# Expert 0's second matrix measured inside the attention, layer 2 in a written order, and 16 identity matmuls ahead of its first rows

## The chip, the core and the metric

The kernel runs on one core of one Trainium2 chip. Its engines are PE (TensorE, the matmuls), DVE (VectorE), ACT (ScalarE), POOL (GpSimd) and SP (SyncE, which here only issues transfers). The metric is the device time of one run in microseconds (us). The profile is one execution, recorded instruction by instruction.

## The reference, cut to what matters

Three stages follow one another: a sparse attention and two mixtures of experts.

```python
# attention: 2 batches, 8 heads, 768 positions, 64 wide, scores kept for 96 local and 8 global positions
scores = scale * q @ k^T + bias;  a = softmax(scores where kept);  x = a @ v      # x: 1536 x 512

# first mixture (called the dense layer): all 8 experts see all 1536 rows, D = 512, F = 1024
P = exp(logits - max)
for _ in range(8):                          # the balancing of the probabilities
    P /= P.sum(1);  P /= P.sum(0);  P *= N / E
out += P[:, e] * (max(x @ w1[e], 0) @ w2[e])          # over e

# second mixture (called layer 2): each expert takes 192 rows, assigned greedily by logit
out[mask_e] = max(x[mask_e] @ w1[e], 0) @ w2[e]
```

## The kernel before

**Numbers and products.** Each float32 operand of the large products is split into two float16 parts, a high and a low one: ACT writes the high part (`split_hi`, L814) and DVE the low one (`split_lo`, L817), both scaled by a power of two that comes from the operand's largest absolute value. A product is then three matmuls (`mm3`, L869 to L871): high by high, high by low, low by high. A matrix of an expert (512 x 1024 or 1024 x 512) must therefore be loaded, measured for its maximum, given a scale, and split before PE can use it. To find a maximum over all partitions, a column of 128 maxima is sent through PE (`spread`, L134, or a transpose of a broadcast column) and reduced.

**Attention.** `band_attention` runs in a written order: inside `with in_order():` each instruction of an engine is tied behind the one before it in the program's text, so that the program's order is the order of the engine's queue. It goes in steps, two per block of 128 rows and 12 blocks. Beside its blocks it runs generators that are asked for one item at fixed places of each step. One of them is `matrices()` (L558), which calls `matrix(0)` (L525): it loads expert 0's first matrix as two transfers of 1 MB into the two buffers of the pool tag `raw`, reduces it in eight parts on DVE (L539, steps 2 to 5), gets its scale by `want_scale` and `broadcast`, and splits it in eight parts on ACT, DVE and POOL (steps 8 to 11). Scores of a step come from PE (`scores`, L595) after DVE's copy of the turned keys into a slab (L584); DVE and ACT then do the softmax (`soften`, L599). From step 13 on, some of expert 0's first products (x by its first matrix) are done inside the attention.

**Between attention and dense layer.** After the attention (about 156 us) the remaining first products of expert 0 follow in nine groups of 12 products of 512 columns each. Behind each group side streams are pumped: small work of other engines (loading, measuring, splitting of weights) is issued in units with a cost for ACT, DVE and POOL. Stream `weights` (L1217) loads expert 0's second matrix in four quarters, measures it in eight parts, four on ACT (`absmax_bound`, L883) and four on DVE (L1202) in `measured`, then settles its scale in `settle` (reduction L1209, spread L134 on PE), and splits it. In the same time the probabilities are balanced on DVE and POOL (L909 to L925). The four quarters of raw space are `quarters`, views of the two `raws`.

**Dense layer.** From 186 us to about 1137 us, in a written order: output products of expert 0 (`out_step`, the 512-column products of L1464), then experts 1 to 7, with the side streams that prepare each next matrix pumped behind fixed groups of products.

**Layer 2.** The dense layer's rows and gate logits give an assignment `inv` of rows to places. The layer's largest absolute value is broadcast by PE (L119), and the rows go out to `xg` in DRAM. Then four pairs of experts follow. For each pair, POOL gathers 384 rows from `xg` (`load_rows`), PE turns them in three sets of four transposes (`turn_rows`, L1956) and ACT and DVE split them. Each expert's first products are four groups of 24 products of 192 columns (`ph`, L869 to L871), evicted by `split_relu` (two passes on ACT, L862 and L863, and one on DVE, L864). Output products (`py`) are 24 products of 512 columns over 8 row blocks f, one per expert and one more for the shared remainder (L2035), each evicted on ACT or DVE and scattered by POOL. PE's groups write to four banks in turn.

Eight of the 16 matrices of layer 2 were split earlier and stored in DRAM (`NPRE = 8`); `fetch` brings them back whole. The other eight are made in layer 2 itself: `make` loads a matrix in eight pieces of 128 x 512 into a ring of five places in `raw2` (POOL issues the first five, SP the others at L1979) and splits each with `split`. This part of the program is not written in a fixed order: the scheduler of the program's builder sets the place of each instruction in each engine's queue.

Of the kernel before, what the change touches and what calls it, by code (L numbers as in the profile page):

```python
# [42 lines left out]
def tile_sparse_attention_moe_moe(ctx, tc, q, k, v, ng, nl, wg1, w11, w12, wg2, w21, w22, out, taps=None):  # L43
# [64 lines left out]

    late = []
# [286 lines left out]
    def band_attention(atp, aps):  # L396
# [161 lines left out]
        def matrices():  # L558
            yield from matrix(0)

# [393 lines left out]
    raws = [rawp.tile([P, WE // 2], F32, name="raw", bufs=2) for _ in range(2)]  # L954
# [262 lines left out]
    def weights(jobs):  # L1217
# [693 lines left out]
    sx2 = pow2_scale(xam[:, NC:], "sx2")  # L1911
    xg = drp.tile([NT, DM], F32)
# [37 lines left out]
    def turn_rows(a):  # L1950
        xr = XR.pop(a)
        x2 = xtp.tile([P, 2, KC, 3 * P], F16, name="xt")
        for z in range(3):
# [4 lines left out]
            last = nc.scalar.activation(hi, pt, AF.Copy, scale=sx2[:, 0:1])  # L1958
            nc.vector.scalar_tensor_tensor(lo, pt, sx2[:, 0:1], hi, op0=ALU.mult, op1=ALU.subtract)
        X2[a] = x2, inv[:, 3 * a:3 * a + 3]  # L1960
        return last

    raw2 = lat.tile([P, NC * DM], F32, name="raw2", tag="acc", bufs=1)
    spare = raw2.bitcast(F16)[:, :2 * 2 * FC * CAP].rearrange("p (z y f t) -> p z y f t", z=2, y=2, f=FC)
    ring = [raw2[:, 2 * FC * CAP + 512 * y:2 * FC * CAP + 512 * y + 512] for y in range(5)]
    turn_ = [0]

    def make(e, which):
        kind, n = seq[USES.index((e, which)) % len(seq)]
        t = pools[kind, n].tile([P, 2, WE], F16, name="w2slot", tag=f"{kind}{n}", bufs=1)  # L1970
        w = (w21, w22)[which][e]
        for a in range(8):
            raw = ring[turn_[0] % len(ring)]
            turn_[0] += 1
            c, h = divmod(a, w.shape[1] // 512)
            if turn_[0] <= len(ring):
# [90 lines left out]
```

## Time and profile before

| | |
|---|---|
| median of 3 runs | 1300.54 us (1300.19 to 1301.31) |
| the profiled execution's own time | 1300.56 us |
| its span, first to last instruction | 1298.8 us |
| PE busy | 1242.9 us, 96% of the span |
| DVE busy | 889.6 us, 68% |
| ACT busy | 754.3 us, 58% |
| POOL busy | 208.6 us, 16% |
| moved by DMA | 211.39 MB, 163 GB/s on average |

Busy time counts what an engine executes, not register, branch, semaphore and transfer-issuing instructions. A share of the span is an average over stages with different limits; the slices and the windows show where an engine was not full. The clock column (PEclk) is TensorE's granted clock, 1.00 being 2.4 GHz and 0.50 being 1.2 GHz; a window in which it changed shows a value between. A row of a window gives its limits and length, then busy us with the count of instructions for PE, PEld (TensorE's weight loads), DVE, ACT and POOL, then the granted clock, the busy share of the DMA engines and GB/s. A row of a timeline gives start, duration, engine, line, operation, tile written <- tiles read, shape and count, and ends, where the engine idled ahead of it, with that idle time and what released it.

### The profile page before, as it was taken

The numbers are of one execution on the slowest core, as the hardware profiler recorded it, in microseconds if no ns is written. First come the engines' busy times: TensorE is split into PE (matmuls) and PEld (weight loads), VectorE is DVE, ScalarE is ACT, GpSimd is POOL, SyncE is SP. The second block draws the span as 40 slices with busy tenths as digits, with TensorE's granted clock in tenths as the row PEclk, the third lists the DMA queues.
The fourth block names the chain that finished last, engine by engine and source line by source line (L and its number), as shares of the span: only waits on it lengthen the run. The fifth ranks groups of instructions, "written<-read, shape, count | busy, mean of one in ns | idle before, by whom it ended". The sixth has DMA issues, their size and how long they took to land.

```text
span 1298.8 us, 24591 instructions
## 1 busy us (share of the span) xinstructions
PE 1242.9 (96%) x9462; PEld 819.7 (63%) x9462; DVE 889.6 (68%) x2038; ACT 754.3 (58%) x1507; POOL 208.6 (16%) x269
## 2 busy tenths in 40 slices
PE   6899989999999999999999999999999999979997
PEld 4666434685478548897468547855785444467665
DVE  7865586777548645878657765776778898836851
ACT  5876453585356435767448645645574676736852
POOL 2543407203001100201100200110000000041100
PEclk9999989999999999999999999999999999989999
DMA  9440023574832473734787674225745233368740
GB/s 243 109 126 14 2 82 130 193 230 163 275 106 74 130 227 128 248 145 152 243 280 238 208 268 148 74 90 182 256 155 196 94 136 128 114 234 286 248 134 25
DMA packets 157445, 211.39 MB, mean 163 GB/s; under 512 B 56528, under 2 KB 91344, under 8 KB 156048
## 3 DMA queue, kind: packets, MB, share of 16 engines
q1 hardware_dynamic: 154720, 198.02, 47.0%
q0 software_dynamic: 2320, 7.60, 1.6%
q10 hardware_dynamic: 288, 4.19, 0.8%
q8 instruction: 74, 1.21, 0.4%
q14 instruction: 43, 0.35, 0.1%
HBM read 176.23 MB, written 33.55 MB: 162 GB/s over the span
## 4 chain that ended last, share of the span: by engine, by line
PE 72%; issue 10%; DVE 9%; ACT 5%; DMA 2%; POOL 2%; POOLq 0%; DVEq 0%; ACTq 0%; SPq 0%
PE pX L1464 11%; PE pY L1490 10%; PE py L1694 8%; PE pX L1490 7%; PE pY L1464 7%; PE pZ L1464 5%; PE pV L1464 5%; PE pV L1490 4%; PE pZ L1490 3%; DMA raw<-in_moe_w_dram 2%; DVE hslot L1511 2%; PE ph L869 1%; PE ph L871 1%; PE ph L870 1%; PE pr L1816 1%
## 5 line engine op out<-in xcount | busy, mean ns | idle before, releaser
L1490 PEld LDWEIGHTS <-ws 128*128 128x128 f16 x3528 | 344.1, 98 | 44.5 <-issue 1.2
L1464 PEld LDWEIGHTS <-hslot 128*128 128x128 f16 x1776 | 172.4, 98 | 199.3
L1464 PE MATMUL pX<-wslot,hslot 128*128 128x512 f16 x768 | 171.5, 379 | 0.0
L1490 PE MATMUL pY<-xs,ws 128*128 128x256 f16 x1008 | 124.7, 273 | 0.5 <-DVE pZ L1570 0.5
L1490 PE MATMUL pX<-xt,ws 128*128 128x256 f16 x1008 | 124.2, 273 | 0.3 <-ACT pY L1539 0.3
L1694 PE MATMUL py<-wslot,hslot 128*128 128x512 f16 x528 | 121.0, 379 | 0.0
L1511 DVE TENSOR_TENSOR hslot<-relu,hslot 128x512 f16<-128x512 f32 x126 | 97.1, 794 | 31.1 <-ACT relu L1504 30.8
L1288 POOL TENSOR_TENSOR raw<-raw 128x512 f32<-128x512 f32 x14 | 22.9, 1633 | 513.3 <-DVE ws L817 222.2
L814 ACT ACTIVATE ws<-raw,s 128x512 f16<-128x512 f32 x98 | 66.3, 714 | 53.8 <-POOL raw L1296 21.7
L1464 PE MATMUL pY<-wslot,hslot 128*128 128x512 f16 x432 | 96.9, 379 | 0.0
L817 DVE SCALAR_TENSOR_TENSOR ws<-raw,s,ws 128x512 f16<-128x512 f32 x98 | 78.0, 821 | 15.7 <-ACT ws L814 15.5
L1694 PEld LDWEIGHTS <-hslot 128*128 128x128 f16 x528 | 49.4, 99 | 60.6 <-issue 8.3
L883 ACT ACTIVATE wide<-raw 128x512 bf16<-128x512 f32 x83 | 52.0, 627 | 44.9 <-DMA raw<-in_moe_w_dram 44.2
L869 PE MATMUL ph<-xt,w2slot 128*128 128x192 f16 x256 | 63.0, 248 | 5.9 <-ACT relu L863 4.8
L1464 PE MATMUL pZ<-wslot,hslot 128*128 128x512 f16 x288 | 64.8, 379 | 0.0
L1464 PE MATMUL pV<-wslot,hslot 128*128 128x512 f16 x288 | 64.8, 379 | 0.0
L1202 DVE TENSOR_REDUCE wam<-raw 128x1 f32<-128x512 f32 x84 | 56.8, 677 | 9.6 <-DMA raw<-in_moe_w_dram 9.4
L870 PE MATMUL ph<-xt,w2slot 128*128 128x192 f16 x256 | 63.0, 247 | 0.0
L871 PE MATMUL ph<-xt,w2slot 128*128 128x192 f16 x256 | 62.9, 247 | 0.0
L1490 PE MATMUL pZ<-xs,ws 128*128 128x256 f16 x504 | 62.7, 272 | 0.0
L1490 PE MATMUL pY<-xt,ws 128*128 128x256 f16 x504 | 62.2, 273 | 0.0
L1490 PE MATMUL pV<-xs,ws 128*128 128x256 f16 x504 | 62.1, 273 | 0.0
(337 smaller groups left out, 2363.2 us busy)
## 6 DMA issues: line engine op xcount, KB each, us to landing
raw<-in_moe_w_dram SPq DMA_DIRECT2D x286, 256.0 KB, 3.6
raw<-in_moe_w_dram SPq DMA_DIRECT2D x64, 512.0 KB, 5.3
relu<-in_moe_w_dram SPq DMA_DIRECT2D x85, 256.0 KB, 4.8
pre<-spill SPq DMA_DIRECT2D x64, 256.0 KB, 4.8
w2slot<-pre SPq DMA_DIRECT2D x6, 2048.0 KB
hd<-hslot SPq DMA_DIRECT2D x12, 512.0 KB, 4.4
hslot<-hd SPq DMA_DIRECT2D x12, 512.0 KB, 5.5
back<-spill SPq DMA_DIRECT2D x16, 256.0 KB, 5.1
```

The lines of the kernel that those rows point to most:

```text
L814: nc.scalar.activation(hi, raw, AF.Copy, scale=s[:, 0:1])
L817: nc.vector.scalar_tensor_tensor(lo, raw, s[:, 0:1], hi, op0=ALU.mult, op1=ALU.subtract)
L869: nc.tensor.matmul(out_, lhs(0, a), rhs(0, a), start=a == 0, stop=False)
L870: nc.tensor.matmul(out_, lhs(0, a), rhs(1, a), start=False, stop=False)
L871: nc.tensor.matmul(out_, lhs(1, a), rhs(0, a), start=False, stop=a == n - 1)
L883: return nc.scalar.activation(t, src, AF.Abs, accum_out=dst)
L1202: nc.vector.tensor_reduce(am[:, a:a + 1], t, axis=AX.X, op=ALU.max, apply_absolute_value=True)
L1288: nc.gpsimd.tensor_tensor(b11, b12, b11, op=ALU.subtract)
L1464: nc.tensor.matmul(flat(ps), h[:, y1, f, t * P:t * P + P], w[:, y2, f, :], start=f == 0 and n == 0, stop=f == FC - 1 and n == 2, skip_grou ...
L1490: nc.tensor.matmul(bank[:, u, :], self.w[:, z1, m, c, u * P:u * P + P], x[:, z2, c], start=first and u == 0 and c == 0 and n == 0, stop=c ...
L1511: nc.vector.tensor_sub(lo, r, hi)
L1694: pin(nc.tensor.matmul(ps, h[:, y1, f, t * P:t * P + P], w[:, y2, f, :], start=f == 0 and n == 0, stop=f == FC - 1 and n == 2))
```

## The change

Three things are changed.

First, the generator `matrices()` goes on after the first matrix: it loads expert 0's second matrix in two transfers into the same two buffers (step 12), reduces it in eight parts on DVE (steps 12 to 16) and asks for its scale. `weights` takes these buffers and this scale over and no longer loads, measures or settles that matrix.

Second, 16 matmuls of the identity by itself (128 x 128 by 512 columns, float16) are pinned behind the broadcast ahead of layer 2. They write to a bank that nobody reads.

Third, layer 2 is put into `in_order()`. The pieces of the last eight matrices go through a ring of six places. A generator `splits()` issues the splitting of one piece at a time, at a rate set by `pace`: 1.25 pieces behind each group of first products, 0.8 behind each row block f of the output products but the last. `need` draws what is still missing of a matrix ahead of its first use, `release` starts the fetch of a stored matrix when its place is free. Pair 0's rows are turned in two parts (`turn_part`): sets 0 and 1 ahead of the first products, set 2 behind the first group. The rest of the layer does the same computation as before; `...` marks what is left out.

```diff
@@ band_attention @@
         def matrices():
             yield from matrix(0)
+            w = w12[0]
+            kc, n = w.shape[0] // P, w.shape[1]
+            wv = w.rearrange("(c p) n -> p c n", p=P)
+            second["raws"] = [pools["raw"].tile([P, WE // 2], F32, name="raw", bufs=2) for _ in range(2)]
+            for z, raw in enumerate(second["raws"]):
+                nc.sync.dma_start(raw.rearrange("p (c n) -> p c n", n=n), wv[:, z * kc // 2:(z + 1) * kc // 2])
+            yield
+            am = sml.tile([P, 9], F32, name="wam4")
+            for y in range(8):
+                part = second["raws"][y // 4][:, y % 4 * (WE // 8):(y % 4 + 1) * (WE // 8)]
+                nc.vector.tensor_reduce(am[:, y:y + 1], part, axis=AX.X, op=ALU.max, apply_absolute_value=True)
+                yield
+            nc.vector.tensor_reduce(am[:, 8:], am[:, :8], axis=AX.X, op=ALU.max)
+            second["s"] = sml.tile([P, 2], F32, name="s2", bufs=3)
+            want_scale(am[:, 8:], second["s"])
+            while not is_known(second["s"]):
+                yield "wait"
...
-    raws = [rawp.tile([P, WE // 2], F32, name="raw", bufs=2) for _ in range(2)]
+    raws = second["raws"] if second else [rawp.tile([P, WE // 2], F32, name="raw", bufs=2) for _ in range(2)]
...
@@ weights @@
-        for a in range(len(quarters)):
-            load(0, a)
-        if not wide:
-            quarters.append(raws[1][:, q4:])
-            load(0, 3)
-            quarters.pop()
-            am = sml.tile([P, 9], F32, name="wam2", bufs=2)
-            for a in range(8):
-                t, begun = loaded[0, a // 2]
-                yield from ready(begun, 16)
-                yield from measured(t[:, a % 2 * 512:a % 2 * 512 + 512], am, a)
-            yield from settle(jobs[0], am, 12)
+        if second:
+            for a in range(4):
+                loaded[0, a] = raws[a // 2][:, a % 2 * q4:(a % 2 + 1) * q4], -LAG
+            scales[jobs[0]] = second["s"]
+        else:
+            for a in range(len(quarters)):
+                load(0, a)
...
@@ ahead of layer 2 @@
     sx2 = pow2_scale(xam[:, NC:], "sx2")
+    warm = mmbank([P, 4, P], name="py")
+    for y in range(16):
+        pin(nc.tensor.matmul(warm, identh, identh[:, None, :].to_broadcast([P, 4, P]), start=y == 0, stop=y == 15))
...
@@ layer 2 @@
-    ring = [raw2[:, 2 * FC * CAP + 512 * y:2 * FC * CAP + 512 * y + 512] for y in range(5)]
+    ring = [raw2[:, 2 * FC * CAP + 512 * y:2 * FC * CAP + 512 * y + 512] for y in range(6)]
...
+    def load_piece(queue):
+
+        if todo:
+            (e, which), y = todo.pop(0)
...
+    def splits():
+
+        last = None
+        for e, which in made:
+            k = USES.index((e, which))
+            while USES[k - len(seq)] not in used:
+                yield
...
+            for y in range(8):
+                yield
+                raw = loads[e, which, y]
+                hi, lo = (t[:, z, y * 512:y * 512 + 512] for z in range(2))
+                split_hi(raw, S2[:, which, e], hi)
+                if last:
+                    split_lo(*last)
+                    load_piece(nc.sync)
+                last = raw, S2[:, which, e], hi, lo
...
+    def pace(x):
+
+        quota[0] = min(quota[0] + x, 2.0)
+        while quota[0] >= 1.0:
+            quota[0] -= 1.0
+            next(pieces, None)
+
+    def need(x):
+
+        while x in made and x not in ready:
+            next(pieces)
+        return W2[x]
+
+    def release(*xs):
+
+        used.update(xs)
+        while fetches and USES.index(fetches[0]) < NPRE and USES[USES.index(fetches[0]) - len(seq)] in used:
+            fetch(*fetches.pop(0))
...
     fetch_next(5)
-    load_rows(0)
-    load_rows(1)
-    st = turn_rows(0)
-    with tc.issue_after(st.ins):
+    with in_order():
+        load_rows(0)
+        load_rows(1)
+        for _ in ring:
+            load_piece(nc.gpsimd)
+        turn_part(0, (0, 1))
         fetch_next(2, nc.scalar)
...
+                    split_relu(ps.rearrange("p a b -> p (a b)"), h[:, 0, f:f + 2, :].rearrange("p a b -> p (a b)"),
+                               h[:, 1, f:f + 2, :].rearrange("p a b -> p (a b)"), 2 * CAP, HS)
+                    if a == 0 and z == 0 and f == 0:
+                        turn_part(0, (2,))
+                    pace(1.25)
+                release((e, 0))
...
+                    if f < FC - 1:
+                        pace(0.8)
```

## Rows read from the trace of the kernel before

**Rows 1.** PE's line in the page's 40 slices, each 32.47 us, busy tenths.

```profile
PE   6899989999999999999999999999999999979997
```

**Rows 2.** Stage table: busy us and count by engine, PEclk, DMA, GB/s.

```profile
200.00:250.00 50.00, 50.00 (x247) 23.92 (x246) 34.46 (x49) 22.12 (x42) 30.75 (x20) 1.00 0.41 136
```

**Rows 3.** Timeline of PE: start, us, line, operation, [wait <-releaser].

```profile
166.54 0.38 PE L871 MATMUL ph<-xt,wslot 128*128 128x512 f16 x1
...
170.98 0.29 PE L134 MATMUL pg<-identh,wam 128*128 128x128 bf16 x1 [4.06 <-DVE wam L1209]
```

**Rows 4.** Half-microsecond windows behind the attention, columns as in rows 2.

```profile
169.00:169.50 0.50, 0.00 (x0) 0.00 (x0) 0.50 (x3) 0.00 (x0) 0.00 (x0) 0.89 0.00 0
...
176.00:176.50 0.50, 0.50 (x3) 0.20 (x2) 0.43 (x3) 0.50 (x1) 0.00 (x0) 0.79 0.00 0
```

**Rows 5.** Chain of waits: start, us, what.

```profile
171.27 0.43 PE ph L869
...
186.08 10.36 PE pX L1464 x48
```

**Rows 6.** Timeline of PE in layer 2: pairs 1 to 3 and the end.

```profile
1187.89 0.26 PE L869 MATMUL ph<-xt,w2slot 128*128 128x192 f16 x1
...
1223.21 0.26 PE L869 MATMUL ph<-xt,w2slot 128*128 128x192 f16 x1
...
1260.57 0.26 PE L869 MATMUL ph<-xt,w2slot 128*128 128x192 f16 x1
...
1276.41 0.38 PE L869 MATMUL py<-w2slot,raw 128*128 128x512 f16 x1
...
1289.70 2.54 PE L2035 MATMUL py<-w2slot,raw 128*64 128x512 f16 x22
```

**Rows 7.** Timeline of PE at the start of layer 2.

```profile
1144.45 0.32 PE L119 MATMUL bc<-ident,xam 128*128 128x128 f32 x1 [1.93 <-DVE xam L1909]
...
1150.03 1.11 PE L1956 MATMUL px<-ident,raw 128*128 128x128 f32 x4 [5.26 <-DMA raw<-xg,inv]
...
1152.95 1.12 PE L1956 MATMUL px<-ident,raw 128*128 128x128 f32 x4 [0.36 <-DMA raw<-xg,inv]
...
1153.86 0.85 PE L869 MATMUL ph<-xt,w2slot 128*128 128x192 f16 x4
```

**Rows 8.** Waits of PE, 1186 to 1250: total us, times, longest.

```profile
PE ph L869 <- ACT relu L863: 4.8, 5, 1.5
...
PE ph L869 <- DVE spill L2040: 1.1, 1, 1.1
```

**Rows 9.** Half-microsecond windows at the start of layer 2, columns as in rows 2.

```profile
1145.50:1146.00 0.50, 0.00 (x0) 0.00 (x0) 0.29 (x2) 0.00 (x0) 0.00 (x0) 0.60 0.00 0
...
1155.50:1156.00 0.50, 0.50 (x7) 0.48 (x5) 0.07 (x1) 0.00 (x0) 0.41 (x1) 0.66 1.44 459
```

**Rows 10.** Timeline of DVE: the balanced probabilities are ready.

```profile
192.91 0.23 DVE L944 TENSOR_SCALAR pf<-PX,of 128x12 f32<-128x12 f32 x1
```

**Rows 11.** Tile raw up to 200 us: ns min/median/max, first, last start.

```profile
L539 DVE TENSOR_REDUCE wam<-raw x8: 667/676/678, 23.9 to 39.8; 128x1 f32<-128x512 f32 x8
```

**Rows 12.** Timelines of DVE and PE in the attention.

```profile
85.97 0.68 DVE L584 COPY slab<-pk 128x512 f32<-128x512 f32 x1
...
88.26 1.05 PE L595 MATMUL ps<-slab,qt 64*128 64x232 f32 x8
```

**Rows 13.** Groups, 1186 to 1252: busy us, mean ns, idle before.

```profile
L817 DVE SCALAR_TENSOR_TENSOR w2slot<-raw,S,w2slot 128x512 f16<-128x512 f32 x56 | 39.9, 748 | 14.0 <-ACT w2slot L814 12.1 <-DMA raw<-in_moe_w_dram 0.8 <-issue 0.5
...
L814 ACT ACTIVATE w2slot<-raw,S 128x512 f16<-128x512 f32 x56 | 38.1, 729 | 12.3 <-DMA raw<-in_moe_w_dram 7.5 <-PE py L2035 3.4 <-issue 1.2
...
L863 ACT ACTIVATE relu<-ph 128x384 f32<-128x384 f32 x16 | 7.9, 492 | 0.0
```

**Rows 14.** Line L1979, 1176 to 1260: loads of pieces, ns and landing.

```profile
L1979 SPq DMA_DIRECT2D raw<-in_moe_w_dram x59: 327/328/1194, 1177.0 to 1246.4; - x59
...
DMA to landing us min/median/max: 2.6/3.6/4.8
```

More of the change, by code (lines that the diff above doesn't have):

```diff
@@ L106, in tile_sparse_attention_moe_moe @@
     nc.vector.memset(ones, 1.0)
+    second = {}
     late = []
@@ L1948, in load_rows, with fetch_next @@
         XR[a] = xr
[L1950 to L1953, printed above, removed]
+    raw2 = lat.tile([P, NC * DM], F32, name="raw2", tag="acc", bufs=1)
+    spare = raw2.bitcast(F16)[:, :2 * 2 * FC * CAP].rearrange("p (z y f t) -> p z y f t", z=2, y=2, f=FC)
+    ring = [raw2[:, 2 * FC * CAP + 512 * y:2 * FC * CAP + 512 * y + 512] for y in range(6)]
+    turn_ = [0]
+    fetches = list(USES)
+    def fetch_next(n, queue=nc.sync):
+        for x in fetches[:n]:
+            fetch(*x, queue)
+        del fetches[:n]
@@ new lines, in tile_sparse_attention_moe_moe @@
+    NA = E // 2
+    made = USES[NPRE:]
+    todo = [(x, y) for x in made for y in range(8)]
+    loads, used, quota = {}, set(), [0.0]
+    def load_piece(queue):
+        if todo:
+            (e, which), y = todo.pop(0)
+            w = (w21, w22)[which][e]
+            raw = ring[turn_[0] % len(ring)]
+            turn_[0] += 1
+            c, h = divmod(y, w.shape[1] // 512)
+            queue.dma_start(raw, w[c * P:c * P + P, h * 512:h * 512 + 512])
+            loads[e, which, y] = raw
+    def splits():
[4 more added lines that the diff above has]
+                yield
+            kind, n = seq[k % len(seq)]
+            t = pools[kind, n].tile([P, 2, WE], F16, name="w2slot", tag=f"{kind}{n}", bufs=1)
+            W2[e, which] = view(t, which)
+            for y in range(8):
[7 more added lines that the diff above has]
+                last = raw, S2[:, which, e], hi, lo
+            yield
+            split_lo(*last)
+            load_piece(nc.sync)
+            last = None
+            ready.add((e, which))
@@ new lines, in tile_sparse_attention_moe_moe @@
+    ready = set()
+    pieces = splits()
+    def pace(x):
[11 more added lines that the diff above has]
+            fetch(*fetches.pop(0))
@@ L1954, in turn_rows, with turn_part @@
+    def turn_part(a, zs):
+        xr = XR[a]
+        if a not in X2:
+            X2[a] = xtp.tile([P, 2, KC, 3 * P], F16, name="xt"), inv[:, 3 * a:3 * a + 3]
+        x2 = X2[a][0]
+        for z in zs:
             pt = aux([P, KC, P], name="px2")
@@ L1957, in turn_rows @@
             hi, lo = (x2[:, y, :, z * P:z * P + P] for y in range(2))
-            last = nc.scalar.activation(hi, pt, AF.Copy, scale=sx2[:, 0:1])
+            nc.scalar.activation(hi, pt, AF.Copy, scale=sx2[:, 0:1])
             nc.vector.scalar_tensor_tensor(lo, pt, sx2[:, 0:1], hi, op0=ALU.mult, op1=ALU.subtract)
[L1960 to L1964, printed above, removed]
@@ L1965, in tile_sparse_attention_moe_moe @@
-    ring = [raw2[:, 2 * FC * CAP + 512 * y:2 * FC * CAP + 512 * y + 512] for y in range(5)]
[L1966 to L1976, printed above, removed]
-                pin(nc.gpsimd.dma_start(raw, w[c * P:c * P + P, h * 512:h * 512 + 512]))
-            else:
-                nc.sync.dma_start(raw, w[c * P:c * P + P, h * 512:h * 512 + 512])
-            split(raw, S2[:, which, e], t[:, 0, a * 512:a * 512 + 512], t[:, 1, a * 512:a * 512 + 512])
-        W2[e, which] = view(t, which)
```

92 lines of the change are left out of this document (43 added, 49 removed).

## The prediction

> **What bounds the kernel now.** I read the 40 slices first, then a stage table, then PE's timeline where a slice is not full. In the slices [rows 1] PE is at 9 nearly everywhere after the first; the dips to read are the sixth slice (162 to 195 us), the 36th (1136 to 1169) and the end. Between 200 and 250 us PE is busy 50.00 of 50 us [rows 2]: the dense layer in the middle (about 186 to 1137 us) is PE's own work in a written order, so what ends earlier before it shifts it whole. I treat it as a block of constant length.
>
> The first dip is one wait. PE's last product of a group starts at 166.54, and the next thing in its queue, the spread of the second matrix's maximum (L134), starts at 170.98, after 4.06 us of waiting for DVE's reduction L1209 [rows 3]. No product behind it needs that maximum; the spread merely stands ahead of them. The stop also costs clock: the granted clock is 1.00 (2.4 GHz) until about 169.4 and half of it (1.2 GHz) from then to about 176.3, 5 us after PE took up work again [rows 4]; meanwhile a 512-column product takes 0.43 us, while 48 of them take 10.36 us (0.216 each) at the full clock [rows 5]. Twelve products fall into the slow part: 12 x (0.43 - 0.216) = 2.6 us. So this place costs 4.06 + 2.6 = 6.6 us, all on the path, because the output products begin at 186.08, right behind the first products [rows 5].
>
> The second place is layer 2, four pairs of experts. First products of the pairs 1, 2 and 3 start at 1187.89, 1223.21 and 1260.57; PE ends at 1292.2 (1289.70 + 2.54) [rows 6]. So pairs 1 to 3 take 35.3, 37.4 and 31.7 us. Pair 3 is the unstalled length but for the 12 transposes that turn the next pair's rows. In pair 0 four of them take 0.9 us at half clock (1152.95 to 1153.86) [rows 7], so twelve take some 1.4 us at the full one. An unstalled pair is then 33.1 us, and pairs 1 and 2 lose 2.2 + 4.3 = 6.5 us. PE's waits in that stretch say where: 4.8 us for ACT's relu in five waits and 1.1 us for a DVE eviction, 5.9 in all [rows 8]. I take 5.9. ACT and DVE are shared there between evictions, which free PE's banks, and the splitting of 64 pieces of the last eight matrices, which nobody needs at once.
>
> The third place is the start of layer 2. PE does one broadcast at 1144.45, then nothing until the gathered rows land at 1150.03; its third set of transposes starts at 1152.95 and the first product at 1153.86 [rows 7]. The clock falls at about 1145.6 and is back at about 1155.8 [rows 9].
>
> **The change, part by part.** (1) Measuring expert 0's second matrix in the attention. It takes away four reductions and four ACT passes behind the attention, with the settle and the spread. What follows in PE's queue are products whose inputs are there, so the 6.6 us go if nothing else is late. Next in line are ACT's evictions into four banks and the split of the matrix, which now starts with the first group instead of after the spread, spread over nine groups of 2.6 us (12 x 0.216). The output products' evictions need the balanced probabilities, which DVE has at 192.91 [rows 10]; products from about 180 on have six banks of 5.2 us, so PE would wait for this only past 211. Nothing else is due.
>
> It adds eight DVE reductions of 0.676 us [rows 11], two in most steps from step 12 of the attention on, and the two transfers. Transfer one goes into the buffer whose reader in the attention is done some steps before; its first reduction comes at about 72 us. Transfer two waits in SP's queue until POOL has read the first matrix's last piece, in step 11; behind it stand the loads of q, k and v, which are needed several steps later. On DVE the reductions stand ahead of the next step's softening and slab copy, and PE's next scores wait for that copy. The tightest place I find is the copy that starts at 85.97 and ends at 86.65, before scores at 88.26 [rows 12]: 1.6 us of room against at most two steps' reductions, 2.7 us, that is 1.1 over. Elsewhere PE is the later one in the step, as it has a group of first products there. Ends: 0 (all under PE's products) and 5.4 (8 x 0.676, none hidden). I take 1.1, as the room in that row decides it. Part (1): 6.6 - 1.1 = 5.5 us earlier, between 1.2 and 6.6.
>
> (2) The 16 matmuls come behind the broadcast at 1144.45 and take 16 x 0.216 = 3.5 to 16 x 0.43 = 6.9 us: they end between 1148.3 and 1151.7, against rows at 1150.03. What they can give: from the first product at 1153.86 to the clock's return at 1155.8 [rows 7, 9] some 12 products run at half clock, at 0.0825 us more each (1.98 us for 24 at the full clock, below), 1.0 us. Whether the clock is up when the rows land is not shown by the trace: now it falls 0.8 us after the broadcast ends [rows 7, 9]. I take half, 0.5, between -0.6 (two sets of 0.9 us at half clock behind 1151.7 end at 1153.5, against the third set's present start at 1152.95) and 1.0.
>
> The Trainium skill (TensorE: Matmul & The Clock Gate, Part 1) says that the default state is the slow clock and that activity releases it. By that rule the 16 matmuls give the full 1.0, and the forecast would be 0.5 us lower; the two rises in the trace, each behind some 5 us of work, agree.
>
> (3) The written order of layer 2. The third part of pair 0's rows is turned after the first group instead of ahead of it: PE can start when the second set is split, which is the third set's time earlier, 0.45 us at the full clock. That I take as 0.4, between 0 and 0.9 (1153.86 - 1152.95). The splitting now has a fixed rate: 1.25 pieces per group of first products, 0.8 per row block of the second. Does it fit under PE? A group is 24 products, 15.84 us / 8 = 1.98 us (1260.57 to 1276.41) [rows 6]. ACT needs two evictions of 0.49 and 1.25 pieces of 0.73: 1.89 us [rows 13]. In an output product of 24 x 0.216 = 5.2 us, 7 x 0.8 = 5.6 pieces take 4.1 us and the eviction 0.7: 4.8. DVE has one eviction per group to ACT's two, and 0.75 per piece. So ACT runs at 92 to 95% of PE's pace, and PE's four banks bridge single waits. Pieces come through a ring of six: split 0.73 + 0.75, issue 0.33 and landing 3.6 (median of 59) [rows 13, 14] make 5.4 us per turn, 0.90 per piece, while the output stage asks for 0.93: just enough, where five buffers gave 1.08. On ACT, an eviction stands behind each piece's wait for its load; on SP, behind the fetch of the eighth stored matrix stand the loads. Gain: 5.9 if no wait is left, 0 if PE waits as now. I take 5.0, leaving 0.9 for late pieces, since the worst landing is 4.8 [rows 14]. The three fetches that move (two on ACT's queue, one on SP's) keep their place after the first transposes and after expert 0.
>
> The Trainium skill (PSUM — Partial Sum Buffer, Engine vs sequencer instructions) calls the queues of ScalarE and VectorE strict FIFO. This speaks against part (3): a piece whose load is late holds every eviction written behind it. Before, ACT's pieces waited 7.5 us for loads in that stretch [rows 13]; if all of that reached PE, part (3) would be -1.6 instead of 5.0.
>
> **The sum.** 5.5 + 0.5 + 0.4 + 5.0 = 11.4 us. The profiled execution took 1300.56 us (span 1298.8 and 1.76 around it), the median of the runs is 1300.54, so it stands for them: 1300.5 - 11.4 = 1289.1 us.
>
> **Rivals.** (a) The attention pays for the measuring: DVE, not PE, sets its steps from 12 to 16, and 4.5 of the 5.4 us show. For it: DVE stands right ahead of the scores. Against: PE is full there, with first products in each step. 1289.1 + 3.4 = 1292.5. (b) The written order gives back its gain: ACT at 95% plus late pieces stall PE as now, about 4.5 of the 5.0 lost: 1293.6. For it: the ring's 3% of room in the output stage. Against: pieces no longer pile up in pairs 1 and 2, pair 3 takes a share. The rule of the Trainium skill on strict queues (PSUM — Partial Sum Buffer, above) is this case. (c) The other side: the ring sets the pace of layer 2. A pair holds some 27 pieces in 33.1 us, 1.23 each; a turn of the ring over 6 x 1.23 = 7.4 us, a landing over 5.6, makes it the bound, and the 54 pieces of two pairs then cost 54 / 6 x (landing - 5.6). From a landing of 6.9 us the gain of 11.4 is gone; at 8 us it costs 21.6, and the kernel takes 1310.7. For it: the gathers, stores and fetches share the queues with the pieces. Against: the worst of 59 landings is 4.8 [rows 14]. (d) The matmuls do not do what they say, the clock is low again when the rows come: 0.5 us lost, 1289.6, inside the forecast. (e) Both (a) and (b): 1297.0.
>
> **Chances and range.** Forecast with (d) 0.60; (a) 0.13; (b) 0.15; (e) 0.04; (c) 0.04; the dense layer's waits for split weights move by more than 2.6 us against the shift, or nothing is left for another reason 0.04. A measurement of this kernel can tell about 0.2%, 2.6 us, from no change. All but the last two are faster: 0.92; same 0.03; slower 0.05. The best case is 6.6 + 1.0 + 0.9 + 5.9 = 14.4, 1286.1; the dense block may add or take 1. The range from 1285 to 1296 takes in (a) and (b).
>
> **What would show it.** Right: no PE gap and no low clock between 156 and 180, the first output product at about 180.6; reductions of the second matrix on DVE between 72 and 100 us, with scores waiting at most about a microsecond; pairs of layer 2 about 33 us apart, PE hardly waiting for relu; ACT's waits on piece loads still there but under PE; the first product of layer 2 some 1.0 us sooner after its first rows. Wrong: DVE waiting at its first reduction for the load; scores waiting 0.5 us or more in each step; PE waits for relu of some microseconds in pairs 1 to 3; a landing above 5.6 us; a dense part whose length differs from before by over 2 us.

## The result, and the profile after

The changed kernel takes 1289.09 us (median of 4 runs, 1287.82 to 1290.9); the kernel before took 1300.83 us in the runs beside it. The ratio is 0.9911, with a 95% interval of 0.9894 to 0.9928: about 0.9% faster. The forecast was 1289.1. Its sum is right, but that it is met so closely is luck: two places missed by 1.84 and 1.39 us in opposite directions, as the rows below and the experiments show.

The profiled execution took 1289.29 us, with a span of 1287.5 us: 11.3 us less than before. PE's line and its granted clock in the 40 slices of 32.19 us:

```profile
PE   6899999999999999999999999999999999979997
...
PEclk9999999999999999999999999999999999999999
```

The sixth slice, which stood at 8 in [rows 1], is a 9 now. The dip in the 36th (1127 to 1159 us) and the end are still there.

**Behind the attention.** PE's timeline, from the broadcast that ends the attention's own work to the first output product, and all that PE waits for from 156 to 190 us (total us, times, longest):

```profile
157.34 0.29 PE L120 MATMUL bc<-ident,gam 128*128 128x128 f32 x1 [0.67 <-DVE logits L695]
...
180.46 9.88 PE L1477 MATMUL pX<-wslot,hslot 128*128 128x512 f16 x45
```

```profile
PE bc L120 <- DVE logits L695: 0.7, 1, 0.7
```

The wait of [rows 3] is gone and no new one has come. The stretch took 29.97 us before (155.94 to 185.91 in PE's timeline) and takes 23.12 now: 6.85 less.

**In the attention.** The tightest place of [rows 12], now with two reductions on DVE ahead of it:

```profile
85.31 1.26 DVE L571 TENSOR_REDUCE wam<-raw 128x1 f32<-128x512 f32 x2
...
88.37 0.68 DVE L602 COPY slab<-pk 128x512 f32<-128x512 f32 x1
...
89.11 0.65 PE L650 MATMUL pe<-ident,ex 128*104 128x128 f32 x4 [0.47 <-DVE slab L602]
...
89.68 1.05 PE L613 MATMUL ps<-slab,qt 64*128 64x232 f32 x8
```

The copy starts 2.40 us later than before and the scores 1.42. Of both, 0.57 us was there before the first reduction: in this execution the scores from the ninth on were late by 0.57 already, as they were in two others (0.4 and 0.55), while in ten kernels with the same code up to there they were on time. What the reductions add is 0.85 us, at these scores and nowhere else. PE's last four transposes ahead of the scores (L650) wait for the copy too and take 0.57 us, so not all of the 1.61 us between the copy's end and the scores in [rows 12] was room.

**The start of layer 2.** PE from the 16 matmuls to the first products, and two half-microsecond windows (the clock is the third number from the end):

```profile
1139.65 3.62 PE L1927 MATMUL py<-identh 128*128 128x512 f16 x16
...
1145.30 0.66 PE L2050 MATMUL px<-ident,raw 128*128 128x128 f32 x4 [2.03 <-DMA raw<-xg,inv]
...
1148.12 0.32 PE L887 MATMUL ph<-xt,w2slot 128*128 128x192 f16 x1 [0.78 <-issue]
...
1148.90 0.32 PE L888 MATMUL ph<-xt,w2slot 128*128 128x192 f16 x1 [0.47 <-DVE xt L2053]
```

```profile
1148.00:1148.50 0.50, 0.32 (x1) 0.10 (x1) 0.40 (x1) 0.07 (x1) 0.29 (x1) 0.62 0.54 205
...
1151.50:1152.00 0.50, 0.50 (x8) 0.50 (x7) 0.00 (x0) 0.00 (x0) 0.50 (x2) 0.97 1.06 418
```

The transposes run at the full clock (0.66 us for four instead of 1.11, [rows 7]). But PE then waits for the splitting of the second set, and the granted clock is at half (1.2 GHz) from 1148.1 to 1151.5, under the first products. From the broadcast (1139.49) to pair 1's first product (1183.42) 43.93 us pass; before it was 43.44 (1144.45 to 1187.89). This place has become slower, although the sign that the prediction gave for it came true: the first product is 2.82 us behind its first rows (1145.30 to 1148.12) instead of 3.83. What was lost lies behind that product.

**Pairs 1 to 3.** First products of the pairs and the last products; then PE's waits from 1140 to 1290, and ACT's waits for pieces there and, in the last line, over the same stretch before (1140 to 1295):

```profile
1183.42 0.26 PE L887 MATMUL ph<-xt,w2slot 128*128 128x192 f16 x1
...
1216.34 0.26 PE L887 MATMUL ph<-xt,w2slot 128*128 128x192 f16 x1
...
1249.25 0.26 PE L887 MATMUL ph<-xt,w2slot 128*128 128x192 f16 x1
...
1275.80 5.13 PE L2106 MATMUL py<-w2slot,raw 128*64 128x512 f16 x46
```

```profile
PE px L2050 <- DMA raw<-xg,inv: 2.8, 2, 2.0
PE ph L887 <- issue: 0.8, 1, 0.8
PE ph L888 <- DVE xt L2053: 0.5, 1, 0.5
```

```profile
ACT w2slot L832 <- DMA raw<-in_moe_w_dram: 7.1, 9, 2.0
...
ACT w2slot L814 <- DMA raw<-in_moe_w_dram: 10.7, 16, 1.7
```

The pairs are 32.92 and 32.91 us apart, the waits for relu of [rows 8] are gone, and ACT still waits 7.1 us for pieces, 10.7 before. From pair 1's first product to PE's end 97.51 us pass instead of 104.35.

The ledger, from rows at each boundary:

| stretch | forecast | measured |
|---|---|---|
| attention, reductions | 1.1 later | 0.85 later (and 0.57 that is not the change's) |
| attention's end to first output product | 6.6 earlier | 6.85 |
| dense layer, first output product to broadcast | 0, within 1 | 0.49 longer |
| broadcast to pair 1 (matmuls 0.5, third set 0.4) | 0.9 earlier | 0.49 later |
| pairs 1 to 3 | 5.0 earlier | 6.84 |
| sum | 11.4 | 11.3 |

### The profile page after: what moved, and what is told of

Its sections match the earlier page's. It is cut to its first block, busy times and chain, and to the rows that moved or that the text cites. A ratio compares the mean times of both kernels' runs of the same rounds, so it can differ in the third digit from the quotient of the medians.

```text
span 1287.5 us, 24598 instructions
## 1 busy us (share of the span) xinstructions
PE 1242.7 (97%) x9478; PEld 821.0 (64%) x9478; DVE 890.5 (69%) x2042; ACT 752.5 (58%) x1499; POOL 210.5 (16%) x270
## 4 chain that ended last, share of the span: by engine, by line
PE 73%; issue 10%; DVE 9%; ACT 5%; DMA 2%; POOL 2%; POOLq 0%; SPq 0%; ACTq 0%; DVEq 0%
PE pX L1477 12%; PE pY L1503 10%; PE py L1707 8%; PE pX L1503 7%; PE pY L1477 7%; PE pZ L1477 5%; PE pV L1477 5%; PE pV L1503 4%; PE pZ L1503 3%; DMA raw<-in_moe_w_dram 2%; DVE hslot L1524 2%; PE ph L887 1%; PE ph L889 1%; PE ph L888 1%; PE pr L1829 1%
```

## The experiments

All times are medians; the ratio is to the kernel before, run beside each. That kernel took 1302.14 us beside the first four experiments, 1301.32 beside the next four and 1301.23 beside the last four, where the expectations start from 1300.5; so a time can lie up to 1.6 us above an expected one for that alone. One kernel's runs lie 1.1 to 5.6 us apart, so a microsecond is read from rows of the profiles, and the time only says whether it fits. Each kernel's boundaries were read from PE's timeline as above.

**The first part alone.** The kernel before, with the second matrix measured in the attention: of the change's diff the places up to and with `weights`.

> The kernel before with the first part of the change alone: the second matrix of expert 0 is measured in the attention; no matmuls of the identity, layer 2 as before. Theory (each part earns its gain at its own place, and the dense layer passes it on whole): the first output product at 180.6 instead of 186.08, the span 5.0 to 5.5 us shorter, 1295.0 to 1295.5; layer 2 keeps its waits for relu of 4 to 7 us, and the attention's end is later by about 0.85 us (the scores at 88.26) and up to 1.4. Rival (the dense layer takes the shift back, because its weights are split by streams that do not move along): the first output product as early, but under 2.5 us left at the end, 1298 or more.

Measured: 1296.71 us, ratio 0.9953 (0.9936 to 0.9971).

```profile
179.93 10.31 PE L1477 MATMUL pX<-wslot,hslot 128*128 128x512 f16 x47
```

```profile
PE ph L887 <- ACT relu L881: 5.4, 4, 2.4
```

```profile
1199.95 0.32 PE L887 MATMUL ph<-xt,w2slot 128*128 128x192 f16 x1 [2.43 <-ACT relu L881]
```

```profile
1200.00:1200.50 0.50, 0.50 (x4) 0.47 (x4) 0.50 (x2) 0.50 (x2) 0.00 (x0) 0.50 1.01 352
```

The first output product is 5.98 us earlier than in the profile before, the scores are 0.85 late from the same place on, and the dense layer passes the gain on (958.91 us from first output product to broadcast, 958.54 before). The end is only 3.9 us earlier, since layer 2, which is unchanged, loses 1.8 us: 0.7 at its start, 1.05 in the pairs. The median is 1.2 us above the theory's range, but 5.4 us below the kernel before run beside it, so the times do not contradict it; the profiles' 3.9 us are less than its 5.0 to 5.5. The rival's place, the dense layer, is excluded. The start's 0.7 us belongs to the clock (table below), and so does the pairs' 1.05: PE waits 0.5 us less for relu and evictions than before (5.4 against 5.9), but the clock is at half from 1199.5 to 1202.9, around the end of the longest of these waits, and what PE does in 3.0 us of that stretch would take 1.5 at the full clock.

**The written order alone.** The kernel before, with the third part and no matmuls: of the diff the part of layer 2.

> The kernel before with the written order of layer 2 alone, with its ring of six; the attention as before, no matmuls of the identity. Theory: the first output product stays at 186.1; pairs 1 to 3 start 33 us apart with no wait of PE for relu, and from the broadcast to the last product 141.5 to 142 us pass instead of 147.8: 1294.5 to 1295. Rival (the two large parts are not independent, the waits in layer 2 come back with other landings of the pieces): PE waits of 2 us or more for relu in pairs 1 and 2, 1297 or more.

Measured: 1295.1 us, ratio 0.9947 (0.9934 to 0.9961). Pairs 1 to 3 take 97.51 us, as in the changed kernel, and PE waits for no relu: the gain of 6.84 us is the third part's own. But the start of layer 2 costs 45.28 us instead of 43.44, so broadcast to last product takes 142.8, not 141.5 to 142:

```profile
1153.15 0.32 PE L869 MATMUL ph<-xt,w2slot 128*128 128x192 f16 x1 [0.78 <-ACT xt L2036]
...
1153.93 0.32 PE L870 MATMUL ph<-xt,w2slot 128*128 128x192 f16 x1 [0.47 <-DVE xt L2037]
...
1157.57 1.06 PE L2034 MATMUL px<-ident,raw 128*128 128x128 f32 x4
```

```profile
1158.50:1159.00 0.50, 0.50 (x6) 0.48 (x5) 0.29 (x1) 0.50 (x2) 0.00 (x0) 0.67 0.51 172
```

The first product comes 3.38 us after the first rows, 0.45 sooner than before, just what the forecast took. But it waits 0.78 us for ACT, the next one 0.47 for DVE, and the clock is low until 1158.8: a whole group and the third set of transposes run at half clock.

**The changed kernel without the matmuls.**

```diff
-    warm = mmbank([P, 4, P], name="py")
-    for y in range(16):
-        pin(nc.tensor.matmul(warm, identh, ...))
```

> The changed kernel without the 16 matmuls of the identity. In the changed kernel they keep the clock up for the first eight transposes (0.66 us for four, before 1.11), but the granted clock falls to half at 1148.1, when the first product starts, and some 16 products run at half clock until 1151.5. Theory (the matmuls only move the slow stretch): the transposes take 0.45 us more per set, but the clock, which starts low then, comes back some 5.8 us after them, at about 1151, so fewer products are slow; the time from the broadcast to pair 1's first product (43.9 us in the changed kernel) changes by less than 0.4 us, and the run stays at 1289 within 0.5. Rival (the prediction's): 0.5 us and up to 1.0 longer, 1289.6 to 1290.1.

Measured: 1290.12 us, ratio 0.9908 (0.9892 to 0.9923). Broadcast to pair 1 takes 45.77 us, 1.84 more than with the matmuls. My theory was wrong, and so was the forecast's value: the matmuls are worth more than both. The clock did not come back 5.8 us after the first transposes (at 1153.0), but 9.5 us after them:

```profile
1147.24 1.11 PE L2047 MATMUL px<-ident,raw 128*128 128x128 f32 x4 [5.51 <-DMA raw<-xg,inv]
```

```profile
1156.50:1157.00 0.50, 0.50 (x7) 0.48 (x5) 0.39 (x2) 0.22 (x1) 0.48 (x1) 0.76 1.02 426
```

The time does not show the 1.84, as it lies within the spread of the runs. The clock's part in it can be seen in every run: the mean granted clock is 0.990 to 0.991 in these four runs, and 0.994 to 0.995 in the four of the changed kernel. The difference of 0.004 over 1290 us is some 10 us at half clock, as much as lies between the two profiles (13.7 us in this one, 3.4 in the changed kernel's; table below).

**More matmuls, up to the first product.**

```diff
-    for y in range(16):
+    for y in range(26):
...
+            if a == 0 and z < 2:
+                n = (3, 6)[z]
+                for y in range(n):
+                    nc.tensor.matmul(warm, identh, ...)
```

> The changed kernel with more matmuls of the identity into the unread bank: 26 instead of 16 behind the broadcast, so that they end about when the first rows land, 3 behind the first set of transposes and 6 behind the second. Theory (the clock falls at 1148.1 because PE stood still for most of the time from 1143.3 on): with PE at work up to the first product the granted clock stays at 1.00, the 16 products at half clock take 0.0825 us each instead of 0.16, and the time from the broadcast to pair 1's first product falls from 43.9 us by 1.2: about 1287.9. Rival (something else holds the clock down there, for instance the start of all engines together): half clock in the same stretch, and the added matmuls cost up to 0.3 us: 1289.1 to 1289.4.

Measured: 1287.52 us, ratio 0.9887 (0.9872 to 0.9903). Broadcast to pair 1: 43.88 us, no gain in the profiled execution.

```profile
1138.50:1139.00 0.50, 0.00 (x0) 0.00 (x0) 0.17 (x1) 0.26 (x2) 0.00 (x0) 0.88 0.39 156
```

```profile
1139.28 7.27 PE L1927 MATMUL py<-identh 128*128 128x512 f16 x26
...
1146.38 0.60 PE L2050 MATMUL px<-ident,raw 128*128 128x128 f32 x4
```

The products do run at the full clock. But here the clock fell ahead of the broadcast, at 1138.9, so the 26 matmuls took 7.27 us instead of 5.6 and the transposes started 7.37 us after the broadcast, where 16 left it at 5.8. From the first transposes to pair 1 it takes 36.5 us instead of 38.1: the theory's gain is there, and the late start takes it back. The profiled execution took 1288.76 us and the other three runs 1287.16 to 1287.6, at or under the theory's 1287.9; what they gained at this place is not shown. A fixed number of matmuls takes a time that depends on the clock it meets.

**The third set ahead again, without and with the matmuls.**

```diff
-        turn_part(0, (0, 1))
+        turn_part(0, range(3))
...
-                    if a == 0 and z == 0 and f == 0:
-                        turn_part(0, (2,))
```

> The changed kernel without the 16 matmuls, and with all three sets of pair 0's rows turned ahead of the first products, as in the kernel before. Without the matmuls alone the time from the broadcast to pair 1's first product was 45.8 us (45.3 in the kernel with the written order alone), against 43.4 in the kernel before: PE stands still between the second set and the first products, and the clock comes back some 9 us after the first transposes instead of 5.8. Theory (the third set filled that gap, and moving it behind the first group cost the clock 3 us): with the third set ahead the clock is back about 5.8 us after the first transposes, and the time falls to 43.5 (43.2 to 44.0), that is 1.8 to 2.3 us less. Rival (the written order itself, or other landings, makes the start slow): 45 or more.

Measured: 1288.28 us, ratio 0.9901 (0.9886 to 0.9916). Broadcast to pair 1: 44.75 us. It lies between theory and rival: 1.0 less than with the third set behind, but not 43.5, as the clock came back 8.1 us after the first transposes.

> The changed kernel with its 16 matmuls, and with all three sets of pair 0's rows turned ahead of the first products. In the changed kernel the time from the broadcast to pair 1's first product is 43.9 us, with half clock from 1148.1 to 1151.5. Theory: the third set fills PE between the second set and the first products, so that the clock does not fall there or falls for a shorter time; the set's own 0.45 us ahead of the products lies beside the splitting of the second set: 42.6 to 43.4, 0.5 to 1.3 us less than now. Rival (the matmuls already give all that there is, and the third set is only later work moved ahead): 43.9 to 44.4.

Measured: 1286.82 us, ratio 0.9894 (0.9879 to 0.991). Broadcast to pair 1: 42.23 us, 1.7 less than in the changed kernel, a little more than the theory's range.

```profile
1148.16 0.25 PE L887 MATMUL ph<-xt,w2slot 128*128 128x192 f16 x1
...
1181.23 0.26 PE L887 MATMUL ph<-xt,w2slot 128*128 128x192 f16 x1
```

No product waits for the splitting of the second set any more, and the clock stays up from the transposes on. That the third set keeps it up is not shown: with the set behind the first group it stayed up in three of five kernels (table below).

**The ring with four places.**

```diff
-    ring = [... for y in range(6)]
+    ring = [... for y in range(4)]
```

> The changed kernel with four places for pieces instead of six. Theory (a turn of the ring, splitting 1.48, issue 0.33 and landing 3.6 us, is 5.4 us, and four places give one piece in 1.35 us, where two pairs need one in 1.23 on average and the output products one in 0.93): ACT's waits for pieces grow to 15 us or more, PE's banks no longer cover them, and pairs 1 and 2 get 2 to 6.5 us longer together: 1291 to 1295.5. Rival (the banks cover any wait of a piece, the number of places does not matter): pairs within 0.3 us of 32.9, 1289.

Measured: 1290.34 us, ratio 0.9921 (0.9907 to 0.9934). ACT's waits for pieces grow from 7.1 to 19.1 us, and PE waits 2.9 us in pairs 2 and 3 (the theory had said 1 and 2):

```profile
ACT w2slot L832 <- DMA raw<-in_moe_w_dram: 19.1, 23, 1.9
```

```profile
PE ph L887 <- DVE spill L2113: 2.9, 2, 1.5
```

From pair 1's first product to PE's end 100.69 us pass, 3.2 more: inside the theory's range, nearer its lower end. So the number of places matters, and six are enough. Five were not tried in the written order, nor six without it. But with four, one less than before the change, 3.66 of the 6.84 us remain, so at least these are not owed to a larger ring.

**A faster pace of the splitting.**

```diff
-                    pace(1.25)
+                    pace(2.0)
...
-                        pace(0.8)
+                        pace(1.28)
```

> The changed kernel with the splitting at 2.0 pieces per group of first products and 1.28 per row block of the output products, instead of 1.25 and 0.8. Theory (the fixed rate is what keeps ACT ahead of PE): in a group ACT then has two evictions of 0.49 and two pieces of 0.73, 2.44 us, against 1.98 of PE, so PE waits for relu 0.4 us or more per group where pieces are at hand, 3 to 8 us in pairs 1 and 2 together: 1292 to 1297. Rival (only the order counts, evictions and pieces being interleaved at all): PE's waits under 1 us, 1289 to 1290.

Measured: 1288.56 us, ratio 0.9909 (0.9893 to 0.9924). PE waits 0.8 us once in the pairs, which take 98.47 us, 0.96 more:

```profile
ACT w2slot L832 <- DMA raw<-in_moe_w_dram: 11.8, 11, 2.1
```

```profile
PE ph L887 <- DVE spill L2113: 0.8, 1, 0.8
```

The rival is right: PE's waits stay under 1 us, and the rate of the splitting hardly matters in this range. ACT waits 11.8 us for pieces instead of 7.1, and the pieces land after 4.1 us in the median instead of 3.0, so the ring probably holds the splitting back before ACT is full; that was only read from these rows.

**One step of the attention without reductions.**

```diff
             for y in range(8):
+                if y == 3:
+                    yield "wait"
```

> The changed kernel with one step of the attention left free of reductions: the fourth and fifth reduction of the second matrix, which stood on DVE at 85.31 behind the scale of batch 0 and ahead of the softening, come one step later, and so do those behind them. In five kernels with the measurement in the attention the steps up to the 16th scores are as before within 0.1 us (0.4 and 0.6 in two executions, already ahead of the first reduction), and then 0.8 us late. Theory (only that step has no room): the lateness stays under 0.2 us, the first output product comes at 179.1 instead of 179.9, the run 0.7 to 0.85 us shorter, 1288.3. Rival (DVE sets every one of these steps, the lateness only shows there): 0.6 us or more late at another step.

Measured: 1286.85 us, ratio 0.99 (0.9886 to 0.9915).

```profile
88.41 1.05 PE L615 MATMUL ps<-slab,qt 64*128 64x232 f32 x8
```

These scores are 0.15 us later than before instead of 0.85, later ones 0.16 at most, and the first output product comes at 179.21 instead of 179.93 (first part alone). Only that step lacked room. The run is 2.2 us shorter than the changed kernel's, more than this: 1.26 us lie at the start of layer 2, where the clock rose early (table below), which this edit does not touch.

**Each reduction twice.**

```diff
-                nc.vector.tensor_reduce(am[:, y:y + 1], part, ...)
+                for _ in range(2):
+                    nc.vector.tensor_reduce(am[:, y:y + 1], part, ...)
```

> The changed kernel with each of the eight reductions of the second matrix done twice: 5.4 us more on DVE in the attention. Theory (DVE has room in most of these steps, none in the step ahead of the 16th scores): that step pays its whole 1.35 us more, the others 0 to 0.7 each: the attention's end 1.4 to 2.7 us later than in the changed kernel, 1290.5 to 1291.8. Rival (DVE is the bound throughout): 4.5 us or more later, 1293.6 or more.

Measured: 1290.77 us, ratio 0.9927 (0.9913 to 0.9941).

```profile
91.59 1.05 PE L614 MATMUL ps<-slab,qt 64*128 64x232 f32 x8
```

The lateness is 0.6 us at the scores before these, 3.3 here and 3.9 at the end, where single reductions left 0.85: 3.0 of the added 5.4 us show. That is 0.3 over the theory's range and well under the rival's 4.5. DVE has room for what the change adds but for one step, and not for twice as much.

**The 16 matmuls alone.** The kernel before, with the second part only: of the diff the three lines behind `sx2`.

> The kernel before with the 16 matmuls of the identity alone; its three sets of rows are turned ahead of the first products. From the broadcast to pair 1's first product it took 43.4 us; without the matmuls, and with all three sets ahead, two other kernels took 44.15 and 44.75, and with both 42.2. Theory (the matmuls keep the clock up through the transposes, and with the third set in the gap through the first products too): 42.2 to 42.8, and the run 0.6 to 1.5 us shorter than before. Rival (the prediction's halfway value): 0.5 us and less, 42.9 to 43.4.

Measured: 1300.39 us, ratio 0.9998 (0.9989 to 1.0007). In the profile broadcast to pair 1 takes 42.47 us instead of 43.44, as the theory had it, and the span is 0.9 us shorter:

```profile
1186.87 0.26 PE L869 MATMUL ph<-xt,w2slot 128*128 128x192 f16 x1
```

The time neither shows this nor excludes it: its interval reaches from 1.4 us faster to 0.9 slower.

**Both amendments.** The third set ahead, and the step without reductions.

> The changed kernel with two amendments: the three sets of pair 0's rows turned ahead of the first products, and one step of the attention left free of reductions. Theory: the two gains add, 1.5 us at the start of layer 2 (42.2 to 42.7 us from the broadcast to pair 1's first product, no half clock from the first transposes on) and 0.8 us in the attention: the first output product at about 179.1, and 1286.0 to 1287.0. Rival (the clock's fall behind the matmuls comes by chance, as it stayed up in one kernel with the third set behind, too): 43.5 or more, 1288.3.

Measured: 1286.93 us, ratio 0.989 (0.9875 to 0.9905). Broadcast to pair 1 takes 42.29 us, and the reductions cost the attention under 0.2 us; its profiled execution has the 0.5 us of lateness ahead of the first reduction that the changed kernel's had. So the first output product comes at 179.75, not 179.1. Each amendment alone had given 1286.8 and 1286.9 us, and the sum of the two is not seen in the time. The rival, chance in the clock's fall, is not settled by one more profile in which it stayed up. All three medians are some 2 us under the changed kernel's, with intervals that overlap its own.

**The start of layer 2 in all kernels.** Times from the broadcast's start, in us, read from PE's timeline and from windows of 0.1 us:

| kernel | third set | matmuls | clock at half | broadcast to pair 1 |
|---|---|---|---|---|
| before | ahead | 0 | 1.2 to 11.5 | 43.44 |
| first part alone | ahead | 0 | -0.7 to 13.0 | 44.15 |
| third set ahead, no matmuls | ahead | 0 | 0.4 to 14.0 | 44.75 |
| written order alone | behind | 0 | 0.9 to 14.6 | 45.28 |
| no matmuls | behind | 0 | 1.7 to 15.4 | 45.77 |
| matmuls alone | ahead | 16 | 0.8 to 4.2 | 42.47 |
| third set ahead | ahead | 16 | 0.2 to 3.6 | 42.23 |
| both amendments | ahead | 16 | -1.0 to 5.8 | 42.29 |
| changed kernel | behind | 16 | 8.6 to 12.1 | 43.93 |
| four places | behind | 16 | -0.1 to 3.3 and 10.2 to 13.6 | 44.48 |
| faster pace | behind | 16 | 1.2 to 4.6 | 42.72 |
| step without reductions | behind | 16 | 1.1 to 4.6 | 42.67 |
| reductions twice | behind | 16 | 0.7 to 4.2 | 42.67 |
| 26 + 3 + 6 matmuls | behind | 35 | -0.1 to 3.3 | 43.88 |

## Why the prediction was right, and where it was not

**Part (1), 5.5 us: right in its steps, the price partly by luck.** The wait and the slow products were put at 6.6 us, and 6.85 went. Nothing came in their place. The tightest place in the attention was the one named, at 85.97 to 88.26 [rows 12]. The price was put at 1.1 us, from two steps' reductions, 2.7, less 1.6 of room; it is 0.85, of 1.83 us by which the copy is later and 0.98 that the room gave. Both terms were put too high, by 0.9 and 0.6 us, and it is partly luck that their difference fits: the room was counted up to the scores, while four transposes ahead of them wait for the copy as well. One step without reductions takes the price away, and doubling shows the next ones. The first part alone gave 5.98 us at the first output product.

**Part (2), 0.5 us: mis-sized.** By the table the 16 matmuls are worth 1.0 us against the execution before, 1.8 against the mean of the three kernels without them and with the third set ahead (44.1 and 42.3), and 2.2 with it behind (45.5 and 43.3). The step that failed is the count of the products at half clock: it took 12 of them from [rows 7, 9], where the clock was back 5.8 us after the first transposes. That was the shortest of five; the other four show 7.1 to 9.5 us. So the upper bound of 1.0 came from one execution that happened to be the best. The rule of the Trainium skill (TensorE: Matmul & The Clock Gate, Part 1), that activity releases the slow clock, pointed the right way: in eight of the nine kernels with matmuls the clock fell about the time of the broadcast and rose while they ran, 3.3 to 5.8 us behind it. The full 1.0 us that the prediction derived from it was still too little, and in two of the five kernels with 16 matmuls and the third set behind the clock was low under the first products all the same.

**Part (3), third set, 0.4 us: wrong sign.** The row was read rightly as far as it went: the first product does come some 0.5 us sooner. The step that failed is to count this as a gain of the whole. PE still has to turn the third set, 0.43 us behind the first group, so its time is moved and not saved; and where it had stood, no product waited for DVE to split the second set. Two kernels whose clock was up under the products show it, the one with the third set ahead:

```profile
1139.00 0.37 PE L120 MATMUL bc<-ident,xam 128*128 128x128 f32 x1 [1.94 <-DVE xam L1922]
```

and the one with a step without reductions, where the set is behind:

```profile
1138.05 0.32 PE L120 MATMUL bc<-ident,xam 128*128 128x128 f32 x1 [1.94 <-DVE xam L1924]
...
1146.68 0.24 PE L889 MATMUL ph<-xt,w2slot 128*128 128x192 f16 x1 [0.78 <-ACT xt L2054]
...
1147.46 0.24 PE L890 MATMUL ph<-xt,w2slot 128*128 128x192 f16 x1 [0.54 <-DVE xt L2055]
...
1149.36 0.60 PE L2052 MATMUL px<-ident,raw 128*128 128x128 f32 x4
```

From the broadcast the first product comes after 8.63 us with the set behind and after 9.16 with it ahead (1148.16 - 1139.00), 0.53 sooner; then 0.54 of wait for DVE and 0.43 for the set follow, that is 0.44 later in all, and 42.67 against 42.23 us is measured. The table's means with the set ahead and behind differ by more: 1.0 us with the matmuls (42.3 and 43.3), 1.4 without (44.1 and 45.5). That goes with how much of the slow stretch lies behind the first product (without the matmuls 2.0 to 4.4 us with the set ahead, 5.7 and 6.2 with it behind); with two to five executions on each side it is not shown how much of this is the set's and how much chance.

**Part (3), waits, 5.0 us: under-sized.** All of the 6.5 us by which pairs 1 and 2 were longer are gone, and 0.3 more: 6.84. The 0.9 us kept back for late pieces was not needed. The working behind it was partly beside the point: ACT at 92 to 95% of PE's pace did not decide, since a pace 1.6 times as high costs 0.96 us. The ring's turn did matter, and with four places it costs 3.2 us.

The Trainium skill calls ScalarE's and VectorE's queues strict FIFO (PSUM — Partial Sum Buffer, Engine vs sequencer instructions), by which a late piece holds the evictions behind it, and this part would give -1.6. Waits of ACT for pieces are there, 7.1 us against 10.7 before over the same stretch (7.5 in the shorter one of [rows 13]), and PE waits for none, which fits banks that cover them; their number was not varied. With four places and 19.1 us of waits, 2.9 reach PE.

**The rivals.** (a) asked for 4.5 us from the attention, and it is 0.85. (b) and (e) did not come. (c) needed landings of 6.9 us; the 58 pieces of the changed kernel that SP loads land after 3.0 us in the median and 4.8 at worst. (d) came in part: the clock was low again under the first products of the changed kernel, but the transposes before them had gained. The sum of 11.4 was met because the pairs gave 1.84 more than forecast and the start of layer 2 1.39 less, which is luck; the other stretches, with the 0.57 us that is not the change's, make up the rest.

## What to carry to other kernels

Work that is moved to a place where its engine has no idle time is not saved; what counts is what it covered where it stood. The third set of transposes covered a wait for the splitting, and moving it made the stretch 0.44 us longer, though the first product came sooner. A cost that hangs on the clock has to be read from several executions; the one profile before happened to be the mildest of five. And where evictions were late behind work that can wait, a written order of the two, with one more place in the ring, removed 6.84 us, while its rate mattered little.

## What the runs showed of the hardware that I had not expected

When the clock falls at the same place of the program differs from one execution to the next: from 1.0 us before the broadcast to 1.7 us after it in kernels whose work up to there is alike, and in the changed kernel not until 8.6 us after it. With the matmuls the clock was low for some 3.5 us (in one kernel twice, in one for 6.8), without them for 10 to 14 us. It can also fall in the middle of the work: in the profile of the kernel without matmuls the dense layer took 961.14 us instead of some 959, and the clock was at half from 556.0 to 559.4 us, where no other profile shows it; PE was busy throughout, so that is 1.7 of the 2 us.

```profile
556.00:556.50 0.50, 0.50 (x4) 0.35 (x3) 0.47 (x2) 0.50 (x2) 0.00 (x0) 0.50 0.00 0
```

Such falls do not explain most of the spread between runs of one kernel, as far as the mean clock of each run tells: of the 15 runs of the kernel before beside the last four experiments, the six with a mean clock of 0.991 took 1299.20 to 1301.63 us, and all 15 took 1299.20 to 1302.47. The third digit of that clock leaves at most some 1.3 us open. What causes the rest is not shown.
